# Scale of the scores moved into the copy of the pooled keys, maximum written negated, one fix-up of the sums moved to ScalarE, and a new order of all steps

## The chip, the cores and the metric

One NeuronCore of one Trainium2 chip. The metric is the device time of one execution in microseconds (us), the median of several runs. In a profile PE is the matrix engine (TensorE), PEld its weight loads, DVE is VectorE, ACT is ScalarE, POOL is GpSimd and SP the engine whose queue issues nearly all DMAs.

## The reference

Inputs: q, k, v of shape 8 x 8 x 576 x 64 (batch, head, position, width), and the weights of a gated layer. All data is float32.

```
k_p = k.reshape(B, H, 72, 8, 64).mean(axis=3);  v_p likewise       # 8 positions pooled into one
scores = (1/sqrt(64)) * q @ k_p^T                                   # 576 x 72 per head
attn = exp(scores - max) ;  attn /= (sum(attn) + 1e-9) ;  o = attn @ v_p
x = o, heads side by side                                           # 8 x 576 x 512
h = relu(x @ w_in);  u, v = two halves of h (512 each)
v_n = (v - mean) / sqrt(var + 1e-6)
v_s[t] = sum_s w_spatial[t, s] * v_n[s] + b_spatial[t]
out = (u * v_s) @ w_out
```

## The kernel before

The eight batches go through the same stages, and the stages of neighbouring batches overlap. A stage is a Python generator that is cut into steps by `yield`; one step issues a few instructions, each to the engine named in it. `ORDER` (line 26) is a written list of 1601 steps. A loop (line 910) walks through it and lets the named stage issue its next step. So the list alone fixes in which order instructions stand in each engine's queue, and in which order SP issues DMAs; every engine works through its queue in order and waits at an instruction whose inputs or buffer aren't ready. There is no planner at run time.

A name such as `1S2~` is batch 1, stage S2, with the variant `~` (a mark stands at the first step of its stage and holds for all of it). The stages of a batch are:

- K: load keys, pool them by sums. In batches 0 and 1 PE pools (line 358, 80 matrix multiplications in three groups: steps 4, 5 and 8) and the copy out of PSUM into `kT` is lines 377 and 382. In the later batches other engines pool, and KT transposes on PE (lines 452 and 453) and copies into `kT` (lines 458 and 462).
- V: load and pool the values (line 401 on PE in batches 0 and 1, copy at line 407, rest at line 502).
- Q0 to Q3: load and transpose the queries of two heads each.
- S0 to S3: scores of two heads on PE (line 597) into one of two PSUM buffers, then softmax: the maximum on DVE (line 559); then either, without a mark, subtraction on DVE (line 567), one exponential on ACT (line 569) and sums on DVE (line 571), or, with `~`, the maximum times -QK on DVE (line 561) and 8 or 10 exponentials on ACT with maximum as bias and a running sum each (line 575). Then, for both, `(sum + 1e-9) * 8` on DVE (line 578), the reciprocal on DVE (line 580), and the product with it on POOL (line 606). 20 of the 32 S stages bear the mark, 5 of them in batches 0 and 1. QK is 1/(8 * sqrt(64)): the 8 is that of the mean of the keys; the factor 8 in line 578 is that of the mean of the values.
- T0, T1, Y0, Y1: transpose the attention weights. Batches 0 and 1 use PE (lines 632 and 637) and copies on ACT; later ones transposes on DVE and two DMAs through HBM. There is one buffer for the result (`pt`).
- P0, P1: attention times values on PE (lines 717 and 724). Its outputs use the same two PSUM buffers as the scores.
- A00 to A13: split that output into a high and a low part (line 174 on ACT, line 176 on DVE), the inputs of the layer.
- v0 to v4, u00 to u13, s00 to s13, o0 to o4: the four products of the layer (lines 778 and 794, 821, 839, 865), their outputs through four PSUM buffers named `mm` which the transposes share.

Names with w (`wv0`, `wu1`, `wo2`, `ws3`) load weights, which arrive as float32 and which DVE (lines 206 to 220), ACT and POOL turn into two parts each; with `^` PE takes part (line 232). They all stand in the first third of the list.

Of the kernel before, what the change touches and what calls it, by code (L numbers as in the profile page):

```python
# [96 lines left out]
def pooled_attention_gmlp(ctx: ExitStack, tc: tile.TileContext, q, k, v, w_in, w_sp, b_sp, w_out, out):  # L97
    nc = tc.nc
# [242 lines left out]

    def first_keys(b, alt):

        copy = nc.vector.tensor_copy if "~" in alt else nc.scalar.copy
        sts = []

        def load(r):
# [593 lines left out]
```

## Time and profile before

| | us |
|---|---|
| median of 3 runs | 552.37 |
| lowest and highest run | 550.41 and 552.52 |
| the profiled execution, its own time | 551.63 |
| its span in the trace | 549.8 |
| PE busy | 526.7 |
| DVE busy | 312.9 |
| POOL busy | 280.8 |
| ACT busy | 246.2 |

The span is what the trace covers; 1.8 us of the profiled execution's time lie around it. Busy time counts each engine alone, and the engines run beside each other, so the busy times don't add up to the span. The granted clock of PE is full outside one stretch near the start.

### The profile page before, as it was taken

To read this page: it belongs to the slowest core of one execution; us is meant where nothing else is said; L and a number is where in the kernel's file an instruction comes from. 1 tells how busy PE (TensorE), PEld (TensorE's weight loads), DVE (VectorE), ACT (ScalarE), POOL (GpSimd) and SP (SyncE) were. 2 spreads that over 40 slices of the span, in tenths; PEclk is the share of its full clock that TensorE was granted. 3 is DMA by queue.
4 is the path that set the end of the run, shared out by engine and by line. 5 is a ranking of instruction groups with operands and counts; after the bars stand their busy time and mean duration, and the time that the engine had idled before them with its cause. 6 is when DMAs were issued, how large, how long until landed. Compare 5 with 4: busy or idle time off the path is not lost.

```text
span 549.8 us, 12189 instructions
## 1 busy us (share of the span) xinstructions
PE 526.7 (96%) x4553; PEld 451.4 (82%) x4553; DVE 312.9 (57%) x720; ACT 246.2 (45%) x813; POOL 280.8 (51%) x391
## 2 busy tenths in 40 slices
PE   4788989999999999999999999999999999999997
PEld 3655867889878987888888897888888988889996
DVE  2997999897935745575563754366324553235110
ACT  2768574554642354443652545237433243134231
POOL 1555485487476775656467265544535144125240
PEclk9969999999999999999999999999999999999999
DMA  7888747436464654645644633713550424100102
GB/s 200 255 203 201 213 89 149 85 66 170 85 178 139 155 158 123 152 97 148 187 97 128 142 105 95 199 41 77 142 118 4 110 61 114 59 0 17 62 0 97
DMA packets 135627, 64.90 MB, mean 118 GB/s; under 512 B 89616, under 2 KB 122384, under 8 KB 135568
## 3 DMA queue, kind: packets, MB, share of 16 engines
q1 hardware_dynamic: 135568, 64.12, 45.8%
q8 instruction: 36, 0.59, 0.4%
q14 instruction: 23, 0.19, 0.1%
HBM read 46.69 MB, written 17.40 MB: 117 GB/s over the span
## 4 chain that ended last, share of the span: by engine, by line
PE 79%; DVE 10%; DMA 3%; POOL 2%; ACT 2%; issue 2%; SPq 1%; DVEq 0%; POOLq 0%; ACTq 0%
PE mm L839 18%; PE mm L821 16%; PE mm L865 16%; PE mm L778 13%; PE s_ps L597 3%; PE o_ps L724 3%; PE mm L794 3%; PE o_ps L717 2%; PE mm L840 1%; PE mm L841 1%; DVE x L215 1%; DMA st<-in_moe_w_out 1%; DVE mx L559 1%; DVE vv L767 1%; DMA out<-ob 1%
## 5 line engine op out<-in xcount | busy, mean ns | idle before, releaser
L821 PE MATMUL mm<-xT,win_h 128*128 128x256 f32 (+1 forms) x512 | 104.7, 298 | 2.4 <-ACT vv L782 1.7
L853 POOL TENSOR_TENSOR gT<-g,gT 128x256 fp32r<-128x256 f32 x64 | 47.7, 750 | 91.4 <-ACT gT L850 91.2
L821 PEld LDWEIGHTS mm<-xT,win_h 128*128 128x128 f32 x512 | 82.9, 188 | 6.9 <-ACT vv L782 2.1
L778 PE MATMUL mm<-win_h,xT 128*128 128x512 f32 x256 | 80.8, 397 | 0.0
L865 PE MATMUL mm<-wout_h,gT 128*128 128x512 f32 (+1 forms) x264 | 80.6, 388 | 0.0
L839 PE MATMUL mm<-wT_h,vn_h 128*128 128x256 f32 (+1 forms) x256 | 76.6, 299 | 0.6 <-ACT ob L869 0.6
L839 PE MATMUL mm<-wT_h,vn_l 128*128 128x256 f32 (+1 forms) x256 | 75.7, 296 | 0.0
L839 PE MATMUL mm<-wT_l,vn_h 128*128 128x256 f32 (+1 forms) x256 | 75.7, 296 | 0.0
L821 PE MATMUL mm<-xT,win_l 128*128 128x320 f32 (+1 forms) x256 | 75.6, 295 | 0.0
L844 DVE TENSOR_TENSOR g<-mm,ru 128x256 f32<-128x256 f32 (+1 forms) x64 | 28.2, 451 | 67.9 <-PE mm L841 55.0
L788 POOL TENSOR_TENSOR vn_l<-vv,vn_h 128x512 fp32r<-128x512 f32 x32 | 42.7, 1343 | 33.2 <-ACT vn_h L786 32.9
L575 ACT ACTIVATE e<-s_ps,mx 128x72 f32<-128x72 f32 x174 | 53.0, 339 | 12.5 <-DVE mx L561 11.3
L865 PEld LDWEIGHTS mm<-wout_h,gT 128*128 128x128 f32 x264 | 48.1, 188 | 10.7 <-issue 1.0
L850 ACT ACTIVATE gT<-g 128x256 fp32r<-128x256 f32 x64 | 26.0, 415 | 67.1 <-DVE g L844 63.5
L778 PEld LDWEIGHTS mm<-win_h,xT 128*128 128x128 f32 x256 | 46.9, 188 | 10.3 <-DVE XR L655 0.5
L176 DVE TENSOR_TENSOR xT<-o_ps,xT 128x256 fp32r<-128x256 f32 (+1 forms) x64 | 28.2, 450 | 40.3 <-ACT xT L174 40.2
L865 PE MATMUL mm<-wout_l,gT 128*128 128x512 f32 (+1 forms) x132 | 51.0, 386 | 0.0
L765 POOL TENSOR_TENSOR rstd<-rstd,small 128x1 f32<-128x1 f32 (+1 forms) x40 | 24.6, 620 | 51.4 <-DVE rstd L763 46.5
L778 PE MATMUL mm<-win_l,xT 128*128 128x512 f32 x128 | 50.5, 395 | 0.0
L839 PEld LDWEIGHTS mm<-wT_h,vn_h 128*128 128x128 f32 x256 | 48.2, 188 | 2.7 <-ACT ob L869 1.0
L839 PEld LDWEIGHTS mm<-wT_h,vn_l 128*128 128x128 f32 x256 | 48.3, 189 | 0.4
L839 PEld LDWEIGHTS mm<-wT_l,vn_h 128*128 128x128 f32 x256 | 48.4, 189 | 0.0
(164 smaller groups left out, 1086.2 us busy)
## 6 DMA issues: line engine op xcount, KB each, us to landing
st<-in_k SPq DMA_DIRECT2D x32, 256.0 KB
qt<-in_q SPq DMA_DIRECT2D x112, 72.0 KB
out<-ob SPq DMA_DIRECT2D x31, 256.0 KB
xd<-X SPq DMA_DIRECT2D x48, 128.0 KB
st<-in_v SPq DMA_DIRECT2D x48, 128.0 KB
pt<-xd SPq DMA_DIRECT2D x24, 256.0 KB
stw<-in_moe_w_in SPq DMA_DIRECT2D x8, 512.0 KB
pt_r<-xdr SPq DMA_DIRECT2D x48, 64.0 KB
```

What stands on the lines that cost most here:

```text
L176: nc.vector.tensor_tensor(lo, src, f32(hi), op=ALU.subtract)
L575: nc.scalar.activation(em[:, h, :], sv[:, h % 2, h // 2, :], AF.Exp, bias=mx[:, h:h + 1], scale=QK, accum_out=sm[:, h:h + 1])
L597: nc.tensor.matmul(s_ps[i * TL:(i + 1) * TL, e, c * SP:(c + 1) * SP], lhsT=lhs, rhs=kT[es, pair, :], start=True, stop=True)
L765: nc.gpsimd.tensor_tensor(rstd[:m], rstd[:m], neg_half[:m], op=ALU.pow)
L778: nc.tensor.matmul(a, lhsT=xT[:, i, o + c * P:o + (c + 1) * P], rhs=w[:, i, DH:], start=(i == 0 and j == 0), stop=(i == NK - 1 and j == 2))
L788: nc.gpsimd.tensor_tensor(t["vn_l"][:, c, :], vv, f32(t["vn_h"][:, c, :]), op=ALU.subtract)
L821: nc.tensor.matmul(a, lhsT=w[:, i, d * P:(d + 1) * P], rhs=xT[:, i, o + ts.start:o + ts.stop], start=(i == 0 and j == 0), stop=(i == NK - ...
L839: nc.tensor.matmul(a, lhsT=x[:, c, ds], rhs=y[:, c, ts], start=(c == 0 and j == 0), stop=False)
L844: nc.vector.tensor_tensor(g, a, t["ru"][:, d, ts], op=ALU.mult)
L850: nc.scalar.activation(dst[:, d, 0, at:at + m], g[:, o:o + m], AF.Copy)
L853: nc.gpsimd.tensor_tensor(dst[:, d, 1, at:at + m], g[:, o:o + m], f32(dst[:, d, 0, at:at + m]), op=ALU.subtract)
L865: nc.tensor.matmul(a, lhsT=src[:, i, x, at:at + m], rhs=w[:, i, cols], start=(i == 0 and j == 0), stop=(i == ND - 1 and j == 2))
```

## The change

Three edits to the arithmetic, none of which changes the matrix multiplications:

1. All copies into `kT` multiply by QK, on ACT or, in the one stage with a mark (`6KT~`), on DVE. The scores then come out scaled, and the exponentials lose `scale=QK`.
2. The maximum is written negated by the reduction itself; the multiplication at line 561 goes, and the subtraction at line 567 becomes an addition.
3. In the marked S stages `sum * 8 + 8e-9` is computed on ACT right behind the exponentials; line 578 on DVE stays for the unmarked stages only.

```diff
+    def scaled_act(dst, src):
+        nc.scalar.activation(dst, src, AF.Copy, scale=QK)
+    def scaled_dve(dst, src):
+        nc.vector.tensor_scalar(dst, src, QK, None, op0=ALU.mult)
     def first_keys(b, alt):
-        copy = nc.vector.tensor_copy if "~" in alt else nc.scalar.copy
+        copy = scaled_dve if "~" in alt else scaled_act
...
-        copy = nc.vector.tensor_copy if alt else nc.scalar.copy
+        copy = scaled_dve if alt else scaled_act
...
-        nc.vector.tensor_reduce(mv, sv, axis=AX.X, op=ALU.max)
-        if alt:
-            nc.vector.tensor_scalar(mx, mx, -QK, None, op0=ALU.mult)
+        nc.vector.tensor_reduce(mv, sv, axis=AX.X, op=ALU.max, negate=True)
...
-            nc.vector.tensor_tensor(ev, sv, mv.unsqueeze(3).broadcast_to(sv.shape), op=ALU.subtract)
+            nc.vector.tensor_tensor(ev, sv, mv.unsqueeze(3).broadcast_to(sv.shape), op=ALU.add)
             yield
-            nc.scalar.activation(em, em, AF.Exp, scale=QK)
+            nc.scalar.activation(em, em, AF.Exp)
...
-                                     AF.Exp, bias=mx[:, h:h + 1], scale=QK, accum_out=sm[:, h:h + 1])
-            yield
-        nc.vector.tensor_scalar(sm, sm, 1e-9, float(POOL), op0=ALU.add, op1=ALU.mult)
+                                     AF.Exp, bias=mx[:, h:h + 1], accum_out=sm[:, h:h + 1])
+            nc.scalar.activation(sm, sm, AF.Copy, bias=1e-9 * POOL, scale=float(POOL))
+            yield
+        if not alt:
+            nc.vector.tensor_scalar(sm, sm, 1e-9, float(POOL), op0=ALU.add, op1=ALU.mult)
```

The list keeps the same 1601 steps with the same marks, and puts them into another order from the first line to the last. Its beginning and its end:

```diff
-    "0Q1^ 0Q0~^ 0K^ 0K wo1~ wo1 0Q0 wv1 0K 0K 0K 0K 0K 0Q0 wo1 0Q1 0Q1 0S1 wo1 0S0 wv1 wv1 0S0 0S0 wv1 wv1 0K 0K wv1 "
-    "0Q3^ 0Q3 0S0 0Q3 0Q2^ wv0~^ 0S1 0S1 0S0 0V 0Q2 0Q2 0S3~ 0S3 0S1 0S1 0S0 wv0 0V 0T0 wv3~ wv1 0V 1K^ 0S2~ 0S3 0S2 "
-    "0S2 wv0 0S3 0V 0V 0V 0S1 wv3 0T0 0Y0 0Y0 0T0 0S2 0V wv3 wv0 wo1 wo1 wv0 0T0 0T0 0T0 wu0 wu0 0S3 1Q0 wu0 wv0 0Y1 "
-    "0P0 0P0 1Q0 wv2~^!% wv2 wv2 1K 0S2 0A01 0P0 0A00 0A00 0A01 0Y1 wu0 wu0 wv3 1K 1K wu1~^ 1K 1K 1K 1Q1 0A10 1K 0A11 "
-    "0T1 1S0~ 0A11 1S0 1K 0T1 0A10 wu1 1Q1 1S1~ 0T1 0T1 0T1 1S0 1S1 0T1 1S0 1S1 wu0 ws4 wu0 ws4 1V^ wv2 wv2 wv2 wv2 "
+    "0Q1^ 0K^ 0K wo1~ 0Q0~^ 0K 0K 0K 0K 0K wo1 wo1 wo1 wv1 0Q1 wo1 wo1 0Q3^ 0Q0 0Q1 0Q0 0S1 0S1 0S0 0S0 wv1 wv1 wv1 "
+    "wv1 0K 0K 0S1 0Q3 0Q3 0S0 0Q2^ 0Q2 0Q2 0S3~ 0S3 0S2~ wv1 wv1 0S1 0S0 0S3 0S0 0S0 0V 0S1 0V 0T0 0V wv0~^ wv0 0V "
+    "0V 0S2 0S2 0S3 0S1 0V 1K^ 0Y0 0Y0 wv3~ wv3 0T0 wv0 0T0 0V wv3 0T0 wu0 wv0 wv2~^!% 1K wu0 1Q0 wu1~^ wv0 0T0 wu0 "
+    "1K 0S3 1K 1K 0T0 wv3 wv3 1Q1 1K 1K 0S2 1V^ 1V 1V wu0 wu0 0P0 0P0 1Q0 wv0 0A00 0A01 0A00 wu0 0P0 0A01 1Q2 1S0~ "
+    "1S0 0S2 0Y1 1K wu0 0T1 wv2 wv2 0T1 0A10 0A10 wu1 0A11 0A11 wv2 0Y1 1Q1 1S0 1S0 1S1~ 1S1 0T1 0T1 1K 1V wv2 wv2 "
...
-    "7s01 7u10 7s10 7s10 7s10 7s11 7s03 7s01 7s11 7s13 7u13 7s13 7s11 7s13 7s01 7s13 6o1 7o0 7o0 7s11 7o2 7o3 7o3 7o0 "
-    "7o2 7o2 7o3 7o1 7o1 7o1 7o4 7o4 7o4 7o2 7o2 7o2 "
+    "7s10 6o3 7s10 7s10 7s10 7s11 7s01 7s01 7s01 7s00 7s02 7s02 7s12 7o4 7s01 7s02 7s00 7s00 7s03 7o2 7o2 7s02 7o4 "
+    "7s00 7o2 7o3 7o3 7o4 7s03 7s03 7s03 7o0 7o3 7o1 7o0 7o0 7o1 7o1 7o2 7o2 7o2 "
```

## Rows read from the trace of the kernel before

**Rows 1.** The page: span, and busy time (share) x instructions of each engine.

```profile
span 549.8 us, 12189 instructions
PE 526.7 (96%) x4553; PEld 451.4 (82%) x4553; DVE 312.9 (57%) x720; ACT 246.2 (45%) x813; POOL 280.8 (51%) x391
```

**Rows 2.** Busy time by stretch: from:to, length, engines, PE clock, DMA share, GB/s.

```profile
0.00:13.70 13.70, 5.89 (x57) 4.64 (x57) 2.89 (x10) 2.80 (x6) 1.87 (x8) 1.00 0.74 200
13.70:110.00 96.30, 85.83 (x1096) 66.75 (x1097) 87.30 (x182) 63.10 (x206) 56.01 (x60) 0.95 0.71 171
110.00:250.00 140.00, 138.65 (x1158) 120.36 (x1157) 91.43 (x210) 62.69 (x221) 94.52 (x133) 1.00 0.52 132
250.00:500.00 250.00, 250.00 (x1948) 216.47 (x1947) 123.75 (x306) 103.14 (x346) 114.67 (x173) 1.00 0.39 99
500.00:549.80 49.80, 46.36 (x300) 43.15 (x299) 7.55 (x14) 14.43 (x36) 13.78 (x19) 1.00 0.14 48
```

**Rows 3.** The same view, the stretch in which PE's clock was lowest.

```profile
27.50:41.20 13.70, 12.02 (x115) 7.03 (x114) 13.05 (x24) 8.50 (x25) 7.05 (x10) 0.67 0.89 203
```

**Rows 4.** Waits of PE: us in total, times, longest.

```profile
PE tp L535 <- DMA qt<-in_q: 5.0, 1, 5.0
PE tp L632 <- POOL e L606: 2.7, 2, 2.1
PE s_ps L597 <- DVE pt_q L548: 1.7, 1, 1.7
PE mm L821 <- ACT vv L782: 1.7, 1, 1.7
```

**Rows 5.** Groups by line: count | busy us, mean ns | idle before.

```profile
L578 DVE TENSOR_SCALAR sm<-sm 128x8 f32<-128x8 f32 (+1 forms) x32 | 11.6, 362 | 3.1 <-ACT e L575 2.6
L561 DVE TENSOR_SCALAR mx<-mx 128x8 f32<-128x8 f32 (+1 forms) x20 | 8.2, 408 | 0.7
L575 ACT ACTIVATE e<-s_ps,mx 128x72 f32<-128x72 f32 x174 | 53.0, 339 | 12.5 <-DVE mx L561 11.3 <-POOL pt_p L606 1.0
```

**Rows 6.** Line 561 alone by stretch: DVE busy (count), clock, DMA share, GB/s.

```profile
0.00:55.00 55.00, 1.68 (x4) 0.91 0.85 215
55.00:110.00 55.00, 0.17 (x1) 1.00 0.57 134
```

**Rows 7.** Timeline of DVE near the start: start, us, line, operation.

```profile
16.80 0.75 DVE L559 TENSOR_REDUCE mx<-s_ps 128x8 f32<-128x576 f32 x1
17.58 0.76 DVE L567 TENSOR_TENSOR e<-s_ps,mx 128x576 f32<-128x576 f32 x1
30.20 0.16 DVE L578 TENSOR_SCALAR sm<-sm 128x10 f32<-128x10 f32 x1
31.74 1.22 DVE L578 TENSOR_SCALAR sm<-sm 128x8 f32<-128x8 f32 x1
```

**Rows 8.** Timeline of POOL beside them.

```profile
21.71 1.04 POOL L606 TENSOR_TENSOR e<-e,rs 128x512 f32<-128x512 f32 x1
31.67 1.26 POOL L606 TENSOR_TENSOR e<-e,rs 128x640 f32<-128x640 f32 x1
```

**Rows 9.** A small copy on ACT: count, ns least/median/most, first and last start.

```profile
L462 ACT COPY kT<-tp x10: 164/181/185, 76.0 to 360.7; 64x32 f32<-64x32 f32 x10
```

**Rows 10.** Timeline of PE near the start; in brackets the idle time before.

```profile
13.89 1.24 PE L597 MATMUL s_ps<-kT,qT 64*64 64x72 f32 x32 [0.74 <-ACT qT L543]
22.81 0.66 PE L632 MATMUL tp<-ident,e 128*128 128x128 f32 x4 [2.05 <-POOL e L606]
23.39 0.73 PE L597 MATMUL s_ps<-kT,qT 64*64 64x72 f32 x32
```

**Rows 11.** The chain that ended last, late in the span: start, us, what.

```profile
299.50 1.13 PE o_ps L724 x16
301.11 2.78 PE mm L778 x12
532.52 13.86 PE mm L865 x72
```

110 rows, old and new, of the table ORDER are left out of this document.

## Prediction

> **What bounds the kernel now.** I read the page first: of a span of 549.8 us PE is busy 526.7, and no other engine above 57% [rows 1]. The busy time by stretch says where the rest lies [rows 2]: PE idles 13.70 - 5.89 = 7.8 us at the start, 96.30 - 85.83 = 10.5 from 13.7 to 110 us, 140 - 138.65 = 1.35 up to 250, nothing from 250 to 500, and 49.80 - 46.36 = 3.4 at the end: 23.1 in all. From 250 us on PE is the bound and nothing in the change takes work from it. Another loss isn't idle time: from 27.5 to 41.2 us the granted clock is 0.67 on average, a mix of the two levels 2.4 and 1.2 GHz, after stretches in which PE had waited again and again; at full clock that stretch would have been worth 13.7 x 0.33 = 4.5 us more [rows 3]. So the change can give at most some 10.5 + 1.35 + 4.5 = 16 us without a shorter start, and what it gives is decided before 110 us. In that part DVE is busy 87.3 of 96.3 us, 91%, and it is the engine on which the softmax of the first batches stands in a queue with the splitting of the weights [rows 2].
>
> The waits of PE name the events [rows 4]: 5.0 us for the first queries, 2.7 for POOL's products of the first softmax, 1.7 for a transpose of queries on DVE, 1.7 for a PSUM buffer that ACT was late to empty.
>
> **The multiplication of the maximum and the fix-up of the sums.** The change takes line 561 off DVE 20 times, 8.2 us, and line 578 from 20 of its 32 places (11.6 us for 32) [rows 5]. Only the part before 110 us can be worth anything. Line 561 runs there 5 times, for 1.68 + 0.17 = 1.85 us [rows 6]. Of line 578 five of the places are marked stages: 1.22 us for one, 0.16 for another [rows 7], and I put the other three at 0.17, as an estimate from the short one: 1.89. Together 3.7 us less on DVE, of 87.3. What that gives PE lies between nothing (DVE is then idle 3.7 us more) and 3.7 (each wait of PE hangs on DVE's queue). I take half, 1.9: of the waits, those for POOL and for DVE's transpose follow on DVE's queue, those for data and ACT don't.
>
> The 1.22 us were not work. The same instruction of 128 x 10 takes 0.16, and over the long one lies a product of POOL, from 31.67 for 1.26 us [rows 7, 8]. So 1.05 us of line 578 and about 1.85 - 5 x 0.17 = 1.0 of line 561 were waiting beside POOL. The Trainium skill says (SBUF — State Buffer, "SBUF: two separate sides") that DVE and GpSimd share one pair of ports as an exclusive lock, held for a whole instruction, and the other blocks. By that rule the next DVE instruction that needs the pair may stand there instead, so 2.05 us of the 3.7 could be handed on; the relief would be 1.7, its half 0.8, and the sum below 1.1 higher. This is the first rival's mechanism.
>
> On ACT come 20 small instructions, right behind the exponentials, and the reciprocal on DVE now waits for them; behind the reciprocal wait POOL's products and then T. The trace has no such instruction; the smallest copy there is 0.164 to 0.185 us [rows 9], an exponential with 72 columns 0.339 [rows 5]. So 0.16 to 0.34 each; I take 0.18, nearest in size. Five of them before 110 us make 0.9 (0.8 to 1.7) on an engine that is busy 63 of 96 us there [rows 2], and each takes the place of an instruction of about 0.17 in the same chain. Net 0, bounds 0 to +1. The Trainium skill (ScalarE: Activation LUTs, "Rules for kernel authors") budgets about 0.3 us per ACTIVATE and says to use VectorE for plain adds and multiplications, which speaks against this move; by it the five would cost 1.5 and the sum would be 0.6 higher.
>
> **The factor in the key copies, the negated maximum.** No instruction is added. A copy with a factor could at most become as long as an exponential, 0.34 against 0.18 [rows 5, 9]; only the copies of batches 0 to 2 lie before 110 us, about 10 instructions, so 0 to +1.6; I take 0, since the factor is an operand of an instruction that is there anyhow. The negation and the addition in place of the subtraction: 0. A reduction with it could only be longer, and I have no row for that.
>
> **The order at the start.** The keys' four first DMAs now go ahead of Q0's four, the key copies stand ahead of wo1 in ACT's queue, but the copy of Q1 stands behind wo1. The first scores started at 13.89 us after 0.74 of waiting for that copy [rows 10]. It could go down by the 0.74 or up by the time in which wo1's data come later than the keys; I take 0, bounds -0.7 to +1.
>
> 0S2 now stands ahead of 0T0. PE waited 2.05 us ahead of 0T0 (start 22.81) and did 0S2 behind it in 0.73 [rows 10]. That fits into the wait: -0.7 (0 to -0.7); it hides as long as 0T0 is the later.
>
> Against it: on DVE the order was maximum of S0, subtraction of S0 (16.80, 17.58 us) [rows 7], then the same for S1. Now it is both maxima, the split of wv1, subtraction of S1, then of S0. S0's stands behind S1's reduction and subtraction, two instructions like S0's of 0.75 and 0.76, and 0T0 needs S0. So 0T0 up to 1.5 later; but its second part needs S1, which is earlier, and the pooling of the values and two key groups of batch 1 now stand between or ahead of 0P0, as work for the wait. I take +0.3, bounds 0 to +1.5.
>
> 1S0 now follows directly on 0P0, whose two output buffers it needs, where 1K's three groups and a transpose stood between. It waits for ACT and DVE to split one half of the output. Bounds 0 and the longest such wait that the trace has on these engines, 1.7 [rows 4]; I take +0.4.
>
> **Behind 110 us.** I added up PE's work between producer and consumer in both lists, with the durations of the chain (2.78 us for a product of v [rows 11]). Between P0 and P1 of a batch, where the one buffer of the transposed weights is refilled, the least for batches 2 to 7 was about 12.6 us and is 15; a product directly behind P1 (as v behind KT, 299.50 and 301.11 [rows 11]) cost nothing, and the list keeps such places. I take half of the 1.35 idle us: -0.7, bounds -1.35 to +1.5. The end is the same: outputs to the last, the half of o2 last (the chain's 13.86 us at one go [rows 11]); 0.
>
> **Sum.** -1.9 + 0 + 0 + 0 - 0.7 + 0.3 + 0.4 - 0.7 = -2.6, and the clock: a PE that waits less may keep its level, or lose it elsewhere; 0, bounds -4.5 to +4.5. The profiled execution took 551.63 us, 1.8 more than its span; so 549.0. The median shown is 552.37, 0.7 above that execution; against it 549.0 is 0.6% less.
>
> **Rivals.** First, nothing to measure. DVE's waits are handed on to the next instruction that meets POOL, the moved scores wait for their buffers, and PE, full from 250 us on, gives nothing: -0.8 - 0.7 + 0.3 + 0.4 + 0.3 = -0.5, so 551.1. For it: the waits of PE for data and ACT (5.0, 1.7) are not DVE's. Against it: DVE at 91%. This is also how it comes out if the added ACT instructions cost their upper bound and eat the relief.
>
> Second, slower: 0T0 comes late. S0's subtraction behind S1's pushes POOL's product and 0T0 by 1.5 us, 0S2 doesn't cover it, and the longer gap brings PE down to 1.2 GHz for another half of such a stretch, 2.2 us; with 1S0's wait at 1.7 it makes 1.5 + 2.2 + 1.7 - 1.9 = +3.5, so 555.1. It decides from where 0T0 starts later than 22.81 + 1.5 = 24.3 us with the score step already done. For it: the low clock came right behind the gaps at 20 to 30 us. Against it: two steps of PE work stand ready for the gap.
>
> Third, the gain is larger, as the clock holds: -2.6 - 2.2, so 546.8; counted with the forecast.
>
> **Numbers.** About 0.5% (2.8 us) is what a measurement of this kernel can tell from no change. Forecast with the third case, faster by more than that: 0.43, at 549.0, own range 545.5 to 549.6. First rival, 0.34. Second rival and other new waits in a list rewritten to the last line: 0.23. The range from 545.5 to 555.5 leaves out about 1 in 10 on each side.
>
> **What would show it.** Right: idle time of PE between 13.7 and 110 us down by some 2 us, with DVE's busy time there down by 3 to 4; line 561 gone; small ACT instructions of about 0.18. 0S2 in the gap ahead of 0T0. Wrong: PE's idle time unchanged or larger with DVE less busy; 0T0 past 24.3 us; a clock below 0.67 or for longer; a wait of PE behind 250 us, of which there is none now. The forecast fails most easily in the clock and in the half that I took of DVE's relief.

## The result, and the profile after

The changed kernel takes 542.52 us (median of 4 runs, 542.29 to 543.72), the kernel before, beside it on the same chip, 551.89: ratio 0.9838, 95% interval 0.9812 to 0.9864. That is 9.4 us less, where 2.6 less was forecast; it lies below the range. Run again later on another chip it took 543.39 (ratio 0.9838, 0.9808 to 0.9869).

The page after: the span, and the busy time and instructions of each engine, as in [rows 1].

```profile
span 540.2 us, 12141 instructions
PE 521.1 (96%) x4553; PEld 447.8 (83%) x4553; DVE 290.9 (54%) x680; ACT 248.4 (46%) x833; POOL 279.3 (52%) x391
```

The span is 9.6 us shorter. PE has the same 4553 matmuls, and yet 5.6 us less busy time: a step that runs at the lower clock, or waits between its own matmuls, counts as busy. The other 4.0 us were idle time. DVE is busy 22.0 us less for 40 instructions fewer.

Busy time by stretch after (columns as in [rows 2]; the last row answers to [rows 3]).

```profile
0.00:13.70 13.70, 6.02 (x65) 4.83 (x69) 3.70 (x11) 3.70 (x7) 2.53 (x9) 1.00 0.83 223
13.70:110.00 96.30, 88.09 (x1165) 69.31 (x1163) 84.51 (x182) 65.32 (x213) 62.37 (x69) 0.95 0.71 174
110.00:250.00 140.00, 140.00 (x1216) 122.27 (x1207) 86.21 (x208) 67.75 (x252) 92.67 (x131) 1.00 0.59 142
250.00:500.00 250.00, 249.90 (x1889) 217.07 (x1888) 112.42 (x271) 100.97 (x336) 111.00 (x169) 1.00 0.36 92
500.00:540.20 40.20, 37.11 (x242) 34.35 (x240) 4.08 (x10) 10.62 (x28) 10.76 (x16) 1.00 0.15 53
27.50:41.20 13.70, 11.85 (x204) 7.92 (x201) 12.04 (x22) 10.05 (x30) 8.77 (x8) 0.87 0.85 197
```

From 13.7 to 110 us PE is idle 8.2 us instead of 10.5, and gets 1165 matmuls done instead of 1096. DVE is still busy 84.5 of these 96.3 us, 2.8 less than before. From 110 to 250 us the 1.35 idle us are gone, and 1216 matmuls stand against 1158. (Matmuls differ in size, so the counts are only a hint.) The mean clock from 13.7 to 110 us is 0.95 as before; only its low stretches lie elsewhere, so 27.5 to 41.2 us looks better (0.87 against 0.67) and 13.7 to 27.5 us worse (0.81 against 1.00). The first record of the clock comes at 18.59 us in the kernel before and at 12.12 after, and ahead of it the view prints 1.00 without a record. The same 32 score products took 1.24 us at 13.89 us before [rows 10] and 0.73 at 13.56 after; 1.24 is also what they take at 39.25 us in the kernel after, repeated, where the granted clock is 0.50.

PE's waits after (total, times, longest), to be laid beside [rows 4]:

```profile
PE tp L364 <- DMA st<-in_k: 5.6, 1, 5.6
PE tp L638 <- POOL e L612: 3.5, 1, 3.5
PE s_ps L603 <- DVE xT L176: 1.9, 1, 1.9
PE s_ps L603 <- ACT qT L549: 1.8, 2, 1.3
PE mm L285 <- DMA st<-in_moe_w_spatial: 0.8, 2, 0.6
```

The first wait is for keys now, not queries, and 0.6 longer; the one for POOL's softmax product grew from 2.1 at the longest to 3.5; one for the split half of an output (DVE, L176) is new at its place, 37.6 us (the kernel before has a wait of 0.8 for the same line, at 163.8 us, and that one is gone). The 1.7 us for DVE's transpose are down to 0.2, and behind 60 us all waits for ACT are gone.

Those last show best in the timeline of PE. First the kernel before, every row from 60 to 110 us with idle time ahead of it (in brackets), then the kernel after, the same stretch:

```profile
70.53 0.56 PE L821 MATMUL mm<-xT,win_h 128*128 128x320 f32 x2 [1.67 <-ACT vv L782]
76.41 0.50 PE L821 MATMUL mm<-xT,win_h 128*128 128x256 f32 x2 [0.73 <-ACT kT L462]
96.44 1.08 PE L637 MATMUL tp<-ident,pt_p 128*32 128x128 f32 x32 [1.44 <-ACT ru L824]
```

```profile
92.60 0.63 PE L285 MATMUL mm<-ident,st 128*128 128x128 f32 x4 [0.63 <-DMA st<-in_moe_w_spatial]
```

3.8 us of waiting for ACT to empty a PSUM buffer became 0.6 us for a transfer. The last of the three stands in each kernel below that keeps the old order there, with the new arithmetic or the old (1.4 to 1.8 us). The first scatters between 0 and 1.67 in them, whatever the arithmetic.

**Where the time went, stretch by stretch of the work.** Windows of clock time shift as soon as one kernel is ahead, so I laid them along PE's work: each shape of matmul gets its mean step from the traces' part behind 250 us (or, where it has too few there, from all), these are added in the order of execution (518 us in all), and the table gives the time that PE took for the same amounts of work, from its first matmul on. It is my reckoning, from the profiled executions, and a single one scatters by 1 to 2 us. With other weights for the shapes that are rare behind 250 us the gain from the first row to the second comes out at 2.5 to 5.9 us in the first column and at 2.1 to 2.7 in the third.

| kernel | work 0 to 50 | 50 to 100 | 100 to 250 | 250 to end |
|---|---|---|---|---|
| before | 66.9 | 53.3 | 153.0 | 268.2 |
| after | 62.1 | 51.1 | 150.5 | 267.8 |
| after, repeated | 64.2 | 51.6 | 150.4 | 268.1 |
| old order, new arithmetic | 65.8 | 53.3 | 155.2 | 268.1 |
| new order, old arithmetic | 65.1 | 52.1 | 151.4 | 268.0 |
| new arithmetic, new order from 100 us | 64.6 | 53.9 | 150.4 | 267.8 |
| new arithmetic, new order from 50 us | 68.3 | 51.4 | 150.4 | 267.9 |
| new arithmetic, new order from 35 us | 65.7 | 51.0 | 150.4 | 267.8 |
| new arithmetic, new order up to 35 us | 64.4 | 53.1 | 153.1 | 268.1 |

Of the gain 2.7 to 4.8 us lie in the first 50 us of work, 1.7 to 2.2 in the next 50, 2.5 in the next 150. In the kernel before the first column ends at 71.9 us, so the wait at 70.53 lies in it, and the two other waits for ACT, 2.2 us, in the second. Behind 250 us of work the rows differ by 0.4 us at most: there it hardly matters in which order the shapes follow each other, the rival that e3 and e4 below name.

### The profile page after: what moved, and what is told of

It reads as the page before. It is cut to its first block, busy times and chain, and to the rows that moved or that the text cites. A ratio compares the mean times of both kernels' runs of the same rounds, so it can differ in the third digit from the quotient of the medians.

```text
span 540.2 us, 12141 instructions
## 1 busy us (share of the span) xinstructions
PE 521.1 (96%) x4553; PEld 447.8 (83%) x4553; DVE 290.9 (54%) x680; ACT 248.4 (46%) x833; POOL 279.3 (52%) x391
## 4 chain that ended last, share of the span: by engine, by line
PE 90%; DVE 4%; ACT 2%; DMA 2%; issue 1%; SPq 0%; POOL 0%; DVEq 0%; ACTq 0%; POOLq 0%
PE mm L845 19%; PE mm L871 18%; PE mm L827 18%; PE mm L784 17%; PE s_ps L603 4%; PE o_ps L730 3%; PE mm L800 3%; PE o_ps L723 2%; PE mm L846 2%; PE mm L847 2%; DMA st_r<-in_k 1%; DVE mx L565 1%; PE mm L407 1%; DMA st<-in_moe_w_spatial 1%; DVE x L206 1%
## 5 line engine op out<-in xcount | busy, mean ns | idle before, releaser
L827 PE MATMUL mm<-xT,win_h 128*128 128x320 f32 (+1 forms) x512 | 104.2, 298 | 0.4 <-ACT vp L413 0.4
L850 DVE TENSOR_TENSOR g<-mm,ru 128x320 f32<-128x320 f32 (+1 forms) x64 | 27.9, 446 | 95.8 <-PE mm L847 87.1
L845 PE MATMUL mm<-wT_h,vn_h 128*128 128x320 f32 (+1 forms) x256 | 77.0, 301 | 0.1
L845 PE MATMUL mm<-wT_h,vn_l 128*128 128x320 f32 (+1 forms) x256 | 75.8, 296 | 0.0
L845 PE MATMUL mm<-wT_l,vn_h 128*128 128x320 f32 (+1 forms) x256 | 75.7, 296 | 0.0
L827 PE MATMUL mm<-xT,win_l 128*128 128x256 f32 (+1 forms) x256 | 75.6, 295 | 0.0
L771 POOL TENSOR_TENSOR rstd<-rstd,small 128x1 f32<-128x1 f32 (+1 forms) x40 | 24.3, 609 | 69.5 <-DVE rstd L769 67.6
L579 ACT ACTIVATE e<-s_ps,mx 128x72 f32<-128x72 f32 x174 | 52.9, 339 | 11.9 <-DVE mx L565 5.9
L827 PEld LDWEIGHTS mm<-xT,win_l 128*128 128x128 f32 x256 | 48.2, 188 | 0.0
```

Of the source, the lines that this page charges most:

```text
L579: nc.scalar.activation(em[:, h, :], sv[:, h % 2, h // 2, :], AF.Exp, bias=mx[:, h:h + 1], accum_out=sm[:, h:h + 1])
L771: nc.gpsimd.tensor_tensor(rstd[:m], rstd[:m], neg_half[:m], op=ALU.pow)
L827: nc.tensor.matmul(a, lhsT=w[:, i, d * P:(d + 1) * P], rhs=xT[:, i, o + ts.start:o + ts.stop], start=(i == 0 and j == 0), stop=(i == NK - ...
L845: nc.tensor.matmul(a, lhsT=x[:, c, ds], rhs=y[:, c, ts], start=(c == 0 and j == 0), stop=False)
L850: nc.vector.tensor_tensor(g, a, t["ru"][:, d, ts], op=ALU.mult)
```

## The experiments

My first theory: the gain is the new order's, since it takes out waits of PE that have nothing to do with DVE. The rivals: the gain is that of the shorter softmax on DVE, or that of the clock.

**One part alone.** All arithmetic edits, with the order of before:

```diff
 ORDER = (                    # the 1601 steps of before
...
-        nc.vector.tensor_reduce(mv, sv, axis=AX.X, op=ALU.max)
+        nc.vector.tensor_reduce(mv, sv, axis=AX.X, op=ALU.max, negate=True)
...
+            nc.scalar.activation(sm, sm, AF.Copy, bias=1e-9 * POOL, scale=float(POOL))
```

> The list of before with the three edits to the arithmetic. Theory A (the order makes the gain; DVE's shorter softmax matters little because PE's long waits are set by what stands where): 550.5 us, 549 to 552, against 551.9 before. Theory B (the shorter softmax on DVE makes it, the order only follows): 545 us, under 547. If both are needed together: about 551, and the list of after with the arithmetic of before also stays above 547.

Measured: 551.03, ratio 0.9991 (0.9968 to 1.0014): nothing. And the new order with the arithmetic of before:

```diff
-ORDER = (                    # the 1601 steps of before
+ORDER = (                    # the 1601 steps of after
...
         nc.vector.tensor_reduce(mv, sv, axis=AX.X, op=ALU.max)
```

> The list of after with the arithmetic of before. Theory A: 543.5 to 545.5 us, as at most 1 to 2 us of the 9.4 are the arithmetic's. Theory B: 548 us or more. Both together needed: 547 to 550.

Measured: 547.1, 0.9914 (0.9887 to 0.994), 5.0 us below the kernel before beside it (552.13). So the order alone gives over half, the edits alone nothing that can be told from none, and both together 3.7 us more than the order alone (547.1 to 543.39, on two chips; by the ratios 4.2). My theory had put the order alone at 543.5 to 545.5, so it missed; the case in which both parts are needed had 547 to 550. Of the three waits for ACT behind 60 us the edits alone keep two (and 53.3 us in the table, as before):

```profile
75.60 0.50 PE L827 MATMUL mm<-xT,win_h 128*128 128x256 f32 x2 [0.75 <-ACT kT L343]
95.64 1.08 PE L643 MATMUL tp<-ident,pt_p 128*32 128x128 f32 x32 [1.45 <-ACT ru L830]
```

The order alone keeps none (52.1).

One place where the edits' relief was lost in the old order, in one execution, shows behind 110 us. First PE in the kernel before, ahead of a score step of a later batch and behind it; then in the kernel with the edits alone:

```profile
163.82 0.73 PE L597 MATMUL s_ps<-kT,qT 64*64 64x72 f32 x32 [0.78 <-DVE xT L176]
165.00 0.31 PE L839 MATMUL mm<-wT_l,vn_h 128*128 128x320 f32 x1
```

```profile
164.12 0.82 PE L603 MATMUL s_ps<-kT,qT 64*64 64x72 f32 x32 [1.86 <-DVE xT L176]
165.81 0.47 PE L845 MATMUL mm<-wT_l,vn_h 128*128 128x320 f32 x1
```

PE came 0.8 us earlier to the same place (162.26 against 163.04) and waited 1.1 us longer for the same split of the attention's output. Then the clock fell too: the same matmul takes 0.47 instead of 0.31, and the rows from 164.6 to 168.0 us show a granted clock of 0.50, the lower level. (This execution took 553.05, 2.0 over its kernel's median, and the clock's share of that stretch is about 1.7 by my reckoning; so the fall is not in the median.) Whether the longer wait is in it isn't shown. The kernel with the new order up to 35 us only (e15, below) has the same list here and the same arithmetic, and its profiled execution, 2.6 us quicker than its kernel's median, waits as long as the kernel before:

```profile
161.12 0.73 PE L603 MATMUL s_ps<-kT,qT 64*64 64x72 f32 x32 [0.74 <-DVE xT L176]
```

So what ate the relief in the old order stays open. In the new order no such wait is left between 110 and 250 us.

**Where in the order.** New arithmetic; the new order up to one point, the old behind it, or the other way round. A hybrid also has a seam, where steps of one list meet the leftovers of the other; it can cost something that neither list has.

```diff
 ORDER = (
+    # e3: steps 1 to 410 of after, then the rest in the order of before
+    # e4: steps 1 to 414 of before, then the rest in the order of after
```

> New arithmetic; the first 410 steps as in the list of after (100 us of PE's work at its steady pace), the rest of the steps in the order of before. Theory A with the gain in the front: PE reaches its 100th us of work at 123 us instead of 130, so some 6.5 us faster than before, 545.5. Rival C (the gain comes from the middle and the end of the list, where PE never waits but changes between shapes more or less often): 550.

> New arithmetic; the first 414 steps as in the list of before, the rest in the order of after. Theory A with the gain in the front: 549, of which the 1.35 us of idle time of PE between 110 and 250 us and the arithmetic are the most. Rival C: 545.

Measured: 549.69 (0.9946, 0.9921 to 0.9972) for the front, and 546.9 (0.9922, 0.9897 to 0.9948) for the back: neither half carries it alone (the theory of a gain in the front had 545.5 and 549, its rival 550 and 545), and the part behind 100 us, for which I had forecast 0.7, gives 4.1 against the edits alone. The front's kernel has a seam: PE waits 2.1 us at 117.6 us. Busy time by stretch of the second one, 110 to 250 us and on, shows no idle time left, with the front as of old:

```profile
13.70:110.00 96.30, 85.56 (x1106) 66.95 (x1107) 87.92 (x176) 64.36 (x211) 56.68 (x62) 0.95 0.71 170
110.00:250.00 140.00, 140.00 (x1237) 122.08 (x1236) 86.26 (x205) 64.78 (x230) 93.61 (x133) 1.00 0.57 142
```

**Which edit.** The changed kernel with the fix-up of the sums back on DVE (e5), and with the maximum written plainly and turned by a multiplication in the marked stages (e6):

```diff
-            nc.scalar.activation(sm, sm, AF.Copy, bias=1e-9 * POOL, scale=float(POOL))
...
-        if not alt:
-            nc.vector.tensor_scalar(sm, sm, 1e-9, float(POOL), op0=ALU.add, op1=ALU.mult)
+        nc.vector.tensor_scalar(sm, sm, 1e-9, float(POOL), op0=ALU.add, op1=ALU.mult)
```

> The kernel after, with the fix-up of the sums of the marked stages back on DVE. With the list of after the three edits together are worth some 4 us (order alone 547.1, both 542.5). If the fix-up carries half or more of it: 544.5 or above. If it is only the place of a small instruction in the same chain (my sum's net 0): 542 to 543.5.

```diff
-        nc.vector.tensor_reduce(mv, sv, axis=AX.X, op=ALU.max, negate=True)
+        nc.vector.tensor_reduce(mv, sv, axis=AX.X, op=ALU.max, negate=not alt)
+        if alt:
+            nc.vector.tensor_scalar(mx, mx, -1.0, None, op0=ALU.mult)
```

> The kernel after, but in the marked stages the maximum is written plain and multiplied by -1 on DVE again. If DVE's queue ahead of 1S0 and the exponentials is what the edits shorten: 544 to 546. If the multiplication was covered: 542 to 543.5.

Measured: 545.68 (0.9889, 0.9831 to 0.9948) and 544.86 (0.9873, 0.9838 to 0.9908). Taken back by themselves the edits cost 2.3 and 1.5 us against the repeat, 3.8 together, which is the 3.7 between the order alone and the whole; but each interval overlaps that of the repeat. The busy time fits that the edits give more here than in the old order, though it doesn't show that this is the reason. DVE's share of the page, for the edits alone, the order alone, and the changed kernel repeated:

```profile
PE 527.3 (96%) x4553; PEld 452.0 (82%) x4553; DVE 299.9 (54%) x680; ACT 250.6 (45%) x833; POOL 282.2 (51%) x391
```

```profile
PE 523.4 (96%) x4553; PEld 449.9 (83%) x4553; DVE 310.6 (57%) x720; ACT 244.4 (45%) x813; POOL 277.4 (51%) x391
```

```profile
PE 522.9 (96%) x4553; PEld 450.0 (83%) x4553; DVE 291.9 (54%) x680; ACT 248.0 (46%) x833; POOL 277.9 (51%) x391
```

In the old order the edits take 312.9 - 299.9 = 13.0 us off DVE, in the new one 310.6 - 291.9 = 18.7. The lines that go were longer there to begin with: line 561, 8.2 us in the kernel before, and line 578, 11.6 [rows 5], in the kernel with the order alone:

```profile
L561 DVE TENSOR_SCALAR mx<-mx 128x8 f32<-128x8 f32 (+1 forms) x20 | 10.8, 541 | 0.7
L578 DVE TENSOR_SCALAR sm<-sm 128x8 f32<-128x8 f32 (+1 forms) x32 | 11.9, 372 | 7.3 <-ACT e L575 6.9
```

What is left of line 578 takes 4.2 us in the repeat and 5.6 with the edits alone.

**The clock.** The gap ahead of 0T0 had grown, and the low clock came behind it. So 24 identity multiplications, whose results are used by nothing, fill that gap in the changed kernel:

```diff
 # ORDER, right behind the first step of 0S2
+    wd0 wd1 wd2 wd3 wd4 wd5   # 4 multiplications of identity by identity each
```

> The kernel after with 24 extra multiplications of the identity by itself (results unused) in PE's queue behind the scores 0S2, in the gap of 3.5 us ahead of 0T0. Theory D (the low clock follows PE's gaps, and its place is worth 1 to 3 us): the low stretch from 22.4 us goes or moves, and the time falls by 1 to 2.5 us, to 540 to 541.5. Rival E (the low clock comes at some time near the start whatever PE does): the same or longer, 542.5 to 545, since the added work runs at half clock and 0T0 is later.

Measured: 543.14 (0.9838, 0.9806 to 0.9871), the same as the repeat without them. (They ran from 20.48 to 25.95 us; the trace has two records for each.) The windows of this kernel, 13.7 to 55 us:

```profile
13.70:27.50 13.80, 13.23 (x247) 12.27 (x241) 11.98 (x24) 9.35 (x37) 10.08 (x13) 1.00 0.87 265
27.50:41.20 13.70, 11.26 (x211) 7.56 (x208) 12.34 (x23) 10.27 (x35) 8.72 (x9) 1.00 0.88 196
41.20:55.00 13.80, 11.47 (x148) 7.58 (x147) 10.35 (x24) 12.35 (x58) 9.50 (x11) 1.00 1.01 265
```

and PE behind the filler in it, then the same steps in the changed kernel:

```profile
25.95 0.60 PE L638 MATMUL tp<-ident,e 128*128 128x128 f32 x4
26.48 1.95 PE L407 MATMUL mm<-st,pairs 128*64 128x256 f32 x16
30.73 1.12 PE L232 MATMUL mm<-x,ident 128*128 128x512 f32 x2
```

```profile
23.70 1.11 PE L638 MATMUL tp<-ident,e 128*128 128x128 f32 x4 [3.50 <-POOL e L612]
24.74 3.68 PE L407 MATMUL mm<-st,pairs 128*64 128x256 f32 x16
30.73 1.13 PE L232 MATMUL mm<-x,ident 128*128 128x512 f32 x2
```

The granted clock stays at 1.00 (2.4 GHz) throughout, the sixteen products of L407 take 1.95 us instead of 3.68, and 0T0 started 2.25 us later; yet L232 comes at 30.73 us in both, and the next waits of PE (2.2 and 1.6 us) took the rest. The time lies in the range of the second theory, but not for its reason: with the gap filled, this execution shows no low clock at all. This run alone leaves open whether the filler's delay ate what the clock gave; e11, below, has half the filler and answers it. The same was done in the kernel before, with 16 multiplications spread over its gap:

```diff
 # ORDER of before: two groups behind the first 0S3, one ahead of each of two parts of 0T0
+    wd0 wd1 ... wd2 ... wd3   # 4 multiplications of identity by identity each
```

> The kernel before with 16 extra multiplications of the identity in PE's gaps ahead of the parts of 0T0. In the list of before the low clock lies on 0P0 and the keys of batch 1. Theory D (that is where 2 to 4 of the 9.4 us went): the low stretches from 28 us go, and the time falls to 548 to 550. Rival E (the chain on DVE, POOL and the data sets it): 551 to 553.

Measured: 551.68 (0.9979, 0.9959 to 0.9999); the clock from 27.5 to 41.2 us went from 0.67 to 0.77, and the time hardly moved.

**The new wait of 1S0.** In the changed kernel PE waits 1.9 us at 37.6 us, last for L176 on DVE; in its repeat 3.1 at 39.2, last for L174 on ACT, the other half of the same split. Here are DVE and POOL near there in the kernel after, then in the repeat, there with ACT and PE too:

```profile
33.44 0.42 DVE L206 TENSOR_SCALAR x<-x 128x512 uint32<-128x512 uint32 x1
33.89 0.69 DVE L215 SCALAR_TENSOR_TENSOR x<-stw,x 128x512 uint32<-128x512 uint32 x1
34.62 1.39 DVE L217 TENSOR_SCALAR y<-x 128x512 uint32<-128x512 uint32 x1
33.95 1.78 POOL L238 TENSOR_TENSOR x<-x,win_h 128x512 f32<-128x512 f32 x1 [4.41 <-ACT win_h L228]
```

```profile
34.26 1.49 DVE L206 TENSOR_SCALAR x<-x 128x512 uint32<-128x512 uint32 x1
35.79 0.69 DVE L215 SCALAR_TENSOR_TENSOR x<-stw,x 128x512 uint32<-128x512 uint32 x1
36.51 0.43 DVE L217 TENSOR_SCALAR y<-x 128x512 uint32<-128x512 uint32 x1
34.20 1.26 POOL L238 TENSOR_TENSOR x<-x,win_h 128x512 f32<-128x512 f32 x1 [3.85 <-ACT win_h L228]
36.51 0.63 ACT L228 ACTIVATE win_h<-x 128x512 fp32r<-128x512 f32 x1 [1.66 <-DVE x L215]
39.25 1.24 PE L603 MATMUL s_ps<-kT,qT 64*64 64x72 f32 x32 [3.13 <-ACT xT L174]
```

Where POOL's product begins first (34.20), the next instruction of DVE, L206, stands beside it for a microsecond (1.49 instead of 0.42), L215 ends late, and ACT waits 1.66 us for it ahead of its splits. Where DVE is ahead by a few hundredths (L215 at 33.89, POOL at 33.95), it is POOL that stands (1.78 instead of 1.26), and then L217, for which ACT doesn't wait. Which of the two it is changes from run to run: in e7 DVE was ahead (34.24 and 34.27) and PE waited 2.2 us; in e15 POOL was first (33.72, L206 at 33.80), and PE waited 3.5. It isn't all of the difference between the two tables: L215 begins 1.90 us later in the repeat, 0.82 of it because DVE reached L206 later, 1.07 because L206 took longer. Three trials to take the wait away: a step of wu0 on ACT put behind the output's split (e8), all four steps of wu0 put behind it (e10), and the latter with 12 identity multiplications in the gap (e11; results unused).

```diff
 # ORDER of after
-    wu0 wu0 0P0 0P0 1Q0 wv0 0A00 0A01 0A00 wu0 0P0 0A01 1Q2
+    wu0 0P0 0P0 1Q0 wv0 0A00 0A01 wu0 0A00 wu0 0P0 0A01 1Q2        # e8
+    0P0 0P0 1Q0 wv0 0A00 0A01 0A00 0P0 0A01 wu0 wu0 wu0 wu0 1Q2    # e10, one wu0 from further ahead
```

> The kernel after with one step moved: the copy of wu0's high part on ACT goes behind the two splits of the output of 0P0. If 1S0's wait of 1.85 us (3.05 and 3.55 in two other runs) comes from ACT standing at that copy, which waits for DVE, which waits for POOL: the wait falls under 1.5 us and the time by up to 1, 541.5 to 542.5. If it is set by PE's output and the splits alone: unchanged, 542.5.

> The kernel after with wu0's four steps on DVE, POOL and ACT moved from ahead of 0P0 to behind the splits of its output. If 1S0's wait is DVE's queue with its 1 to 1.4 us beside POOL (the splits stood at 36.75 us on DVE while ACT had been done): the wait falls to 1 us or less and the time by 0.5 to 1.5, 541 to 542. If that wait only moves on to 1S1 or the values: unchanged, 542 to 543.5.

> The same with 12 extra multiplications of the identity in the gap ahead of 0T0, 24 having been too many (0T0 2.2 us later). If the full clock is worth something once DVE lets 1S0 start: 539.5 to 541. If the chain on DVE and POOL sets P0 and the rest anyhow: 541 to 543, like the run without them.

> The kernel after, unchanged, as the measure for the runs beside it: 542 to 543.7.

Measured: 543.5 (0.9845, 0.9809 to 0.988), 544.34 (0.9857, 0.9824 to 0.989), 544.43 (0.9862, 0.9826 to 0.9897), against 543.39 (0.9838, 0.9808 to 0.9869) for the unchanged repeat. In e8 the wait was 2.5 us, not under 1.5. In e10 and e11, which came out above both ranges that I had given them, it went down to 1.1 us as meant. In e10 PE's waits for POOL's product became two:

```profile
PE tp L638 <- POOL e L612: 6.5, 2, 3.5
PE s_ps L603 <- DVE xT L176: 1.1, 1, 1.1
```

The second of them is 3.0 us, at 42.1. The wait moves on; it isn't this step that costs.

The pair e10 and e11 also answers what e7 left open. PE near 0T0 in e10, then with the 12 multiplications in e11:

```profile
24.27 3.69 PE L407 MATMUL mm<-st,pairs 128*64 128x256 f32 x16
30.41 1.12 PE L232 MATMUL mm<-x,ident 128*128 128x512 f32 x2
```

```profile
24.76 1.95 PE L407 MATMUL mm<-st,pairs 128*64 128x256 f32 x16
29.34 1.08 PE L643 MATMUL tp<-ident,pt_p 128*32 128x128 f32 x32 [1.43 <-ACT vp L413]
30.35 1.12 PE L232 MATMUL mm<-x,ident 128*128 128x512 f32 x2
```

Here the filler hardly delays anything, L407 runs at the full clock, and PE then stands 1.43 us until ACT has copied its sums (L413, behind ACT's exponentials). L232 comes at 30.35 instead of 30.41, and the time is the same. In these 40 us PE arrives where DVE, POOL and ACT let it.

**Still open: where the order's gain begins.** New arithmetic throughout, the change-over at 50 us (e13) and at 35 us (e14), and the new order only up to 35 us (e15):

```diff
 ORDER = (
+    # e13: steps 1 to 222 of before, then the rest in the order of after
+    # e14: steps 1 to 146 of before, then the rest in the order of after
+    # e15: steps 1 to 157 of after, then the rest in the order of before
```

> The three arithmetic edits, the old order for the first 222 steps (to about 50 us), the new order behind. If the gain of the order lies in the waits of PE on ACT between 64 and 97 us (1.66, 0.73 and 1.44 us idle in the kernel before), they are gone here and the time is 543.0 to 545.0. If it lies in the front (the first 50 us), the time is 546.0 to 547.5, as with the new order behind 100 us alone (546.9).

> The three arithmetic edits, the old order for the first 146 steps (to about 35 us), the new order behind. Theory that the waits behind 50 us carry the gain: 542.5 to 544.5, within 1 us of the one that changes over at 50 us. Theory that the first steps (second scores ahead of 0T0) carry it: 546 or more.

> The three arithmetic edits, the new order for the first 157 steps (to about 35 us), the old order behind. Theory that the waits behind 50 us carry the gain: 550 to 552, no faster than the edits alone (551.0), with the waits of PE on ACT between 64 and 97 us still there. Theory that the front carries it: 546 to 548.

Measured: 548.6 (0.9937, 0.9917 to 0.9958), 545.21 (0.9882, 0.9854 to 0.991), 551.64 (0.9995, 0.9977 to 1.0013). The first lies above the ranges of both theories: the waits for ACT are gone from it (51.4 in the table), but there is a seam, with two new waits of PE at 70.0 and 72.5 us, 2.7 us together, and the lower clock behind them (68.3 for the first 50 us of work). The second has no such seam: 5.8 us of the 7.6 between the edits alone (551.03) and the repeat (543.39) lie behind 35 us. It lands between the two theories, above 544.5 and below 546, and 3.4 us from the first, where the theory had wanted 1; the missing 1.8 against the repeat would be the front's, but the two intervals overlap. The third is as the theory had it: the new front by itself is worth nothing (its profiled execution, 549.02, was its quickest).

## Why the prediction was wrong

Its side was right, its size 6.8 us short. The step that failed is the price of the order: -0.7 in the sum, -5.0 by itself as measured (e2). I followed the moved steps that I had seen at the front, let the idle time stand for all that could be won behind 110 us, and gave most waits of PE no term. The half that I took of DVE's relief failed beside it. Its signs of being right nearly came in all the same (PE's idle time from 13.7 to 110 us down by 2.3 us, DVE's busy time there by 2.8), but they look only at the part where I had put the whole gain. Term by term:

- **DVE's relief, forecast -1.9 of a possible 3.7.** Mis-sized, and for a reason: there was no one value to find. In the old order the relief gave -1.1 by the medians (552.13 to 551.03; -0.5 by the ratio, with none inside the interval), in the new one -3.7. That this equals the upper end that I had named is in part chance: I had allowed a gain before 110 us alone, and about 0.9 of it lies between 100 and 250 us of work (151.4 against 150.5).
- **The waits beside POOL.** The first rival gave 1.1 us to a handing-on. The trace agrees with the Trainium skill (SBUF — State Buffer, "SBUF: two separate sides"), by which one of DVE and GpSimd holds a shared pair of ports for a whole instruction while the other blocks, in single places: L206 1.49 for 0.42, L217 1.39 for 0.43. But removed waits were hardly handed on. In the new order the removed lines were 10.8 + 11.9 - 4.2 = 18.5 us of DVE, and its busy time fell by 18.7; in the old one 8.2 + 11.6 - 5.6 = 14.2 and 13.0. The rival's condition, DVE no less busy, didn't come.
- **ACT's additions, forecast 0 at 0.18 us each.** Right: 20 instructions of 208 to 216 ns,

```profile
L581 ACT ACTIVATE sm<-sm x20: 208/210/216, 23.9 to 379.1; 128x8 f32<-128x8 f32 x13, 128x10 f32<-128x10 f32 x7
```

  (count, then least, median and most in ns). The Trainium skill (ScalarE: Activation LUTs, "Rules for kernel authors") budgets about 0.3 us for an ACTIVATE whose bias is a pointer operand, which this one's is not, and sends plain additions to VectorE; here the row is 0.21, and moving it back to DVE cost 2.3 us by the medians (e5), with overlapping intervals. So the engine that was not full was no worse a place; that it was the better one isn't shown.
- **Key copies and the negated maximum, forecast 0.** Right: L565 takes 804 ns in the median and 706 to 910 (line 559 before: 808, 719 to 910), the small key copies 186 on average (before: 179 in line 462 and 180 in line 382).
- **The start, 0 (-0.7 to +1).** Right: the first scores begin at 13.56 us instead of 13.89 [rows 10].
- **0S2 in the gap, -0.7, and 0T0, +0.3.** The step did go into the gap, and 0T0 came at 23.70, +0.9, inside the bound of 1.5. In the repeat it came at 24.5 us, past the 24.3 from which the slower rival was to decide, and with the filler at 25.95; the time stayed 543. That rival's price was wrong: neither the lateness of 0T0, up to 2.25 us, nor the clock behind it showed in the time.
- **1S0's wait, +0.4, bound 1.7.** Mis-sized: 1.9 to 3.1. It didn't show in the time: brought down to 1.1 (e10), it gave nothing.
- **Behind 110 us, -0.7 (-1.35 to +1.5).** Mis-sized: -2.5, and the idle time was a bad bound. PE took 153.0 us there for 150 of work, and only 1.35 of the 3.0 were idle; the rest counts as busy, and went too (150.5); what it was made of isn't shown. Of the 2.5 the order by itself gave 1.6. The premise that all is decided before 110 us was wrong.
- **No term at all** for the waits of PE for ACT from 64 to 97 us, 3.8 us idle. I had the longest as a row [rows 4] and set it down as a wait that the relief of DVE doesn't touch. So far as the runs tell, that was so: with the new arithmetic in the old order 2.2 to 3.1 us of them are left (e1 and e15 have two, e4 all three), and with the old arithmetic and a filler 2.7 (e12). But the other part of the change, the order, does touch them, and there I only followed the steps that I had seen moved at the front, and the second half of the list.
- **The clock, 0 (-4.5 to +4.5).** Right in the value; e7 and e11 show it to be worth about nothing here, and e12, in which part of the low stretch went, agrees; so the 4.5 us were no part of what could be won, nor of the range.

Summed: the order, -0.7 forecast, is -5.0 by itself; the relief, -1.9 forecast, is -3.7 on top of it, together the 8.7 of the repeat (543.39 against 552.05 for the kernel before beside it). The order's own, by the profiled executions: about -1.8 in the first 50 us of work, -1.2 and -1.6 in the next two parts and -0.2 behind (rows "before" and "new order, old arithmetic" of the table). Not settled is what each moved step in the front gives, since hybrids cut there have seams of their own, and why the edits gave so little in the old order.

## What to carry to other kernels

An order and the durations that it was made for belong together: the same shorter softmax gave 1.1 us at best guess in the old order and 3.7 in the new. To price a rewritten order, go through all of the bottleneck engine's waits one by one and ask of each whether its producer now stands earlier, instead of following only the moved steps that catch the eye; and count waits inside busy steps too, by laying both kernels along the engine's work rather than along the clock. Before paying for the clock, look whether PE or its suppliers set the pace in that stretch: here it was the suppliers, and the full clock gave nothing.

## What the runs showed of the hardware

A clock that could be kept at 2.4 GHz gave no time: the filler brought L407 from 3.68 to 1.95 us and the next common step to the same 30.73, and half the filler brought L407 from 3.69 to 1.95 and PE to a wait of 1.43 us for ACT. And a race of a few hundredths of a microsecond between DVE and POOL (DVE's L215 at 33.89 and POOL at 33.95 in one run, POOL at 34.20 and DVE's L206 at 34.26 in the next) decides which of DVE's instructions stands for 1.0 to 1.1 us; PE's wait near 38 us was 1.9 us in the one and 3.1 in the other.
